# Cosformer attention and a token-channel mixer on one core: first fills in quarters, w_ch1 in rows, the start of w_ch2 in halves

## The chip, the cores and the metric

One core of a Trainium2 chip. The metric is the device time of one execution in microseconds (us); lower is better. The engines are named as in the profile: PE (TensorE, products) with PEld (its weight loads), DVE (VectorE), ACT (ScalarE), POOL (GpSimd), and the queues of SP (SyncE) and POOL that issue DMAs. Inputs and output are float32 in the chip's main memory (HBM); the products run in bfloat16.

## The reference

```python
# q, k, v: (8, 8, 576, 64)
theta = pi / 2 * arange(S) / S
phi(x) = concat([relu(x) * cos(theta), relu(x) * sin(theta)], -1)
kv = einsum('bhsf,bhsd->bhfd', phi(k), v)
z = sum(phi(k), axis=2)
num = einsum('bhsf,bhfd->bhsd', phi(q), kv)
den = einsum('bhsf,bhf->bhs', phi(q), z)[..., None] + 1e-6
x = (num / den), heads side by side        # (8, 576, 512)

h = relu(x.T @ w_tok1) @ w_tok2            # 576 -> 256 -> 576, over tokens
u = x + h.T
out = u + relu(u @ w_ch1) @ w_ch2          # 512 -> 1536 -> 512, over channels
```

## The kernel before

**Tiling.** A sequence of 576 rows is four chunks of 128 rows (row 4p + r of a head lies in partition p, chunk r) and a tail of 64; the tails of two batches share one tile. A batch has a front (features of k and q, the values with a column of ones, key-value products, numerators, the token mixer) and a channel part (`Channel`: `c_main` multiplies by w_ch1 into `c_ps`, ACT applies ReLU into `h1T`, `o_step` multiplies by w_ch2 into `o_ps`, DVE adds u, SP stores). The channel part of batch b runs through a list of steps, and `pieces` gives the pieces of the front of the next batch, each with the step behind which it is put. Nothing is reordered afterwards: each engine executes its instructions in the order in which the program writes them, and waits by semaphores.

**The first front.** Batch 0 has no channel part to lie beside, so `first_front` is written out by hand. It opens with `busy(idle_ps, 12)`: twelve products of the identity with zeros, 512 columns each, whose result nobody reads. Then, for heads 0 to 3 and again for heads 4 to 7, four chunks of q become features and are transposed on PE (`q_trans`, L343), with one such filling product behind each group of four transposes. More of them follow beside the k sums (`ksum`, L287). Then come key-value products (L323), denominators (`dens`, L303), numerators (`num_half`, L371), first token products (`tok1`, L394), transposes of x (`turned_x`, L437) and the second token products (`turned_b`, L444). It ends with the first three blocks of w_ch1's product for batch 0 (`c_block`, L572), with the four blocks of the 512 contraction rows in the outer loop. Every product on PE is two instructions, a weight load and the product.

**The first loads.** SP and ACT load q, k and v of batch 0, and SP the two token weights (as `u_sb` in the profile, since they are staged in buffers of that name). GpSimd loads the weights that are cast on the way to bfloat16: the tail rows of w_tok1 (L185), w_ch1 in four pieces (L190; two halves of its columns, each in two pieces of 256 rows), of which the first waits for k of batch 0, and w_ch2 in three thirds (L198). In the profile both channel weights are called `w_ch`. The loads of batch 1 (k, v, q, each with its tail) are issued by SP, and the first of them waits for w_ch1's second piece. k and q of batch 2 wait for w_ch2's second third.

**Batch 1's front beside batch 0's channel part.** The plan of `pieces` for the first case names, behind step 8, value casts on ACT and GpSimd (`values`, L276 and L278) and the loads of w_ch2:

```python
(8, V, 2, pool), (8, load_w_ch2, 0), (8, V, 3, pool),
(8, load_w_ch2, 1), (8, load_w_ch2, 2), (9, V, 1, act), (9, QS, 0)]
```

V is a value cast, QS the features of a chunk of q. Behind step 11 come the key-value products of batch 1 and the transposes of the first q chunks (QT). The output products of batch 0 follow: chunks 0 and 1 take turns over w_ch2's thirds, two contraction blocks in a step.

Of the kernel before, what the change touches and what calls it, by code (L numbers as in the profile page):

```python
# [16 lines left out]
def kernel(  # L17
# [15 lines left out]
    nc = tc.nc  # L33
# [5 lines left out]
    Dm2, D_ch = moe_w_ch1.shape  # L39
# [143 lines left out]
        nc.gpsimd.memset(t[half(1)], 0.0)  # L183
    for g in range(2):
        nc.gpsimd.dma_start(out=w_tail1[half(g), :], in_=moe_w_tok1[SM:S, :])  # L185
    C2 = D_ch // 2
    w_ch1_done = []
    for c2 in range(2):
        for ki in range(0, NCC, 2):
            w_ch1_done.append(nc.gpsimd.dma_start(  # L190
                out=w_ch1[:, ki:ki + 2, c2 * C2:(c2 + 1) * C2],
                in_=moe_w_ch1[ki * P:(ki + 2) * P, c2 * C2:(c2 + 1) * C2]
                .rearrange("(n c) d -> c n d", c=P)))
    after(w_ch1_done[0], k_done)
    w_ch2_done = []
    def load_w_ch2(third):
        ki = third * NCH // 3
        w_ch2_done.append(nc.gpsimd.dma_start(  # L198
            out=w_ch2[:, ki:ki + 4, :].rearrange("t (a n) d -> t a n d", n=2),
            in_=moe_w_ch2[ki * P:(ki + 4) * P, :].rearrange("(a t n) d -> t a n d", t=P, n=2)))  # L200

    def busy(dst, times):
        for _i in range(times):
            nc.tensor.matmul(dst, ident, zeros[:, 0:dst.shape[-1]], start=True, stop=True)

    def cast_tok1(mi):
        nc.scalar.copy(w_tok1[:, :, mi * P:(mi + 1) * P], w_tok1n[:, :, mi * P:(mi + 1) * P])
# [8 lines left out]
    class Front:  # L218
# [253 lines left out]
        def pieces(self, b, before):  # L472

            first, odd, late = b == 1, b % 2 == 1, b == 2
            V, KV, N = self.values, self.kv, self.num
            KS, QS, QT, T = self.k_side, self.q_side, self.q_trans, self.tok2
            C, O = 0, NCH
            if first:  # L480

                u, act, pool = before.tok2, nc.scalar, nc.gpsimd
                plan = [(2, u, 0, ps_at, False), (2, u, 1, ps_at, False), (3, u, 2, ps_at, False),
                        (4, KS, 0), (4, u, 3, ps_at, False), (5, KS, 1),
                        (5, u, R, ps_at, False), (5, KS, 2, True), (6, KS, 3, True), (7, KS, R),
                        (7, V, R, nc.vector), (8, V, 0, act),
                        (8, V, 2, pool), (8, load_w_ch2, 0), (8, V, 3, pool),
                        (8, load_w_ch2, 1), (8, load_w_ch2, 2), (9, V, 1, act), (9, QS, 0)]
                plan += [(11, KV, ci) for ci in range(NSC)]
                plan += [(11, QS, 1), (11, QS, 2, True), (11, self.kv_out),  # L490
                         (11, QT, 0, (0, H), act, ps_at), (11, QT, 1), (11, QS, R),
                         (O, QT, 2), (O, N, 0), (O, QS, 3), (O + 1, QT, R),
                         (O + 1, N, 1), (O + 3, N, 2), (O + 3, QT, 3),
                         (O + 5, N, R), (O + 7, N, 3), (O + 8, before.tail_cast)]
            else:
                if late:
                    plan = [(C + 5, V, 1, nc.vector), (C + 5, V, 3, nc.vector),
                            (C + 6, V, 0, nc.scalar), (C + 6, V, 2, nc.scalar),
                            (C + 7, V, R, nc.scalar)]
                else:  # L500
                    plan = [(C + at, V, ci, nc.scalar)
                            for ci, at in enumerate((-1, -1, 0, 1, 2))]

                if odd:
                    sides = ((-4, KS, 0), (-3, QS, 0), (0, KS, 1), (0, KS, 2), (1, QS, 1),
                             (1, KS, 3), (1, QS, 2), (2, QS, 3))
                elif late:
                    sides = ((-4, KS, 0), (-3, KS, 1), (0, KS, 2), (1, KS, 3), (1, QS, 0),
                             (2, QS, 1), (3, QS, 2), (4, QS, 3), (5, KS, R), (9, QS, R))
                else:  # L510
                    sides = ((-4, KS, 0), (-3, KS, 1), (0, KS, 2), (1, KS, 3), (1, QS, 0),
                             (2, KS, R), (2, QS, 1), (3, QS, 2), (4, QS, R), (5, QS, 3))
                for at, side, ci in sides:
                    plan.append((C + at, side, ci))
                    if side == QS:
                        plan.append((C + at, self.q_trans_dma, ci))

                plan += [(C + at, KV, ci) for ci, at in
                         enumerate((7, 7, 8, 8, 8) if late else
                                   (2, 3, 4, 5, 6) if odd else (2, 3, 4, 6, 7))]  # L520
                plan.append((C + (8 if late else 6 if odd else 7), self.kv_out))
            if first:
                at, mix, t = (), O + 7, O + 11
            elif odd:
                at, mix, t = (C + 8, C + 9, C + 10, C + 11, O + 2), O + 3, O + 7
            elif late:
                at, mix, t = (C + 10, C + 11, O + 1, O + 2, O + 4), O + 5, O + 9
            else:
                at, mix, t = (C + 9, C + 10, C + 11, O + 1, O + 3), O + 4, O + 8
            plan += [(i, N, ci) for i, ci in zip(at, ORDER)]  # L530
            plan += [(mix, self.mix_head, 0), (mix + 1, self.mix_head, 1),
                     (mix + 2, self.mix_tail)]

            plan += [(t + at, T, ci) for ci, at in enumerate((0, 1, 2, 3, 3) if not first else
                                                             (0, 0, 1, 2, 2))]
            plan += [(t + 3 - first, self.u_trans_dma, 3, R)]
            plan.append((t + 2 - first, self.u_trans_dma, 0, 3))
            if odd:
                plan.append((t + 3 - first, self.tail_trans_dma))
            slots = {}  # L540
            for slot, what, *args in sorted(plan, key=lambda p: p[0]):
                slots.setdefault(slot, []).append((what, args))
            return slots
# [109 lines left out]
    def first_front(f):  # L653
# [1 line left out]

        idle_ps = ps_at.tile([P, 2, 512], F32, name="idle_ps", tag="at")[:, 0, :]
        lo_heads, hi_heads = (0, HH), (HH, H)
        busy(idle_ps, 12)

        for j in range(2):  # L660
            f.feature("q", 3, j, lo_heads, on_act=True)
        for heads in (lo_heads, hi_heads):
            for ci in range(R):
                if (heads, ci) != (lo_heads, 3):
                    f.feature("q", ci, 0, heads)
                    f.feature("q", ci, 1, heads)
                f.q_trans(ci, heads)
                busy(idle_ps, 1)
        f.q_side(R)
        f.q_trans(R, pool=ps_at)  # L670
        busy(idle_ps, 2)
# [98 lines left out]


    results = [dict() for _ in range(B)]
    load_batch(1, "kvq", behind=w_ch1_done[1])
    tails = {0: tail0}
    fronts = {0: Front(0, results[0], tail0)}

# [8 lines left out]
    for b in range(B):  # L785
# [4 lines left out]
        for i, step in enumerate(steps):  # L790
# [3 lines left out]


            if b == 0 and i == NCH:
                load_batch(2, "kq", behind=w_ch2_done[1], tails=False)
            if b == 0 and i == NCH + 13:
                load_batch(2, "v")
                load_batch(2, "k", main=False)  # L800
# [46 lines left out]
```

## Time and profile before

| | |
|---|---|
| median of 3 runs | 268.46 us (267.81 to 268.73) |
| profiled execution | 268.86 us, of which the span from first to last instruction is 267.1 us |
| PE busy | 260.8 us of the span, 2,063 products |
| DVE, ACT, POOL busy | 165.7, 128.0, 12.6 us |
| granted PE clock | full in all 40 slices |
| DMA | 53.68 MB, mean 201 GB/s |
| last output product ends | 263.9 us; the rest is the last addition and store |

The profile is one execution. A group's line gives its start, its length, the engine, the line of the program, the operation, the buffers and how many instructions; in brackets stands the idle time ahead of it and what ended it. "Issue" means that the engine waited for nothing that the profile shows. PE's products are pipelined: one of 512 columns lasts 0.38 us in the list, but the next begins 0.216 us after it. In the DMA view q1 is the queue that SP's loads and stores use, q0 the one of GpSimd's, and q8 carries instructions; each line has packets, megabytes and the share of the 16 DMA engines. A DMA's time is from its issue to its landing, when its semaphore tells of it.

### The profile page before, as it was taken

To read this page: it belongs to the slowest core of one execution; us is meant where nothing else is said; L and a number is where in the kernel's file an instruction comes from. 1 tells how busy PE (TensorE), PEld (TensorE's weight loads), DVE (VectorE), ACT (ScalarE), POOL (GpSimd) and SP (SyncE) were. 2 spreads that over 40 slices of the span, in tenths; PEclk is the share of its full clock that TensorE was granted. 3 is DMA by queue.
4 is the path that set the end of the run, shared out by engine and by line. 5 is a ranking of instruction groups with operands and counts; after the bars stand their busy time and mean duration, and the time that the engine had idled before them with its cause. 6 is when DMAs were issued, how large, how long until landed. Compare 5 with 4: busy or idle time off the path is not lost.

```text
span 267.1 us, 5160 instructions
## 1 busy us (share of the span) xinstructions
PE 260.8 (98%) x2063; PEld 139.6 (52%) x2063; DVE 165.7 (62%) x381; ACT 128.0 (48%) x227; POOL 12.6 (5%) x26
## 2 busy tenths in 40 slices
PE   7989999999999999999999999999999999999995
PEld 2665466465644455446644455446644455445544
DVE  6974888785565846876565846776565846720022
ACT  4963795428506362546516362546606372526500
POOL 6420140000000000000000000000000000000000
PEclk9999999999999999999999999999999999999999
DMA  6999998869998999469994989279964560180023
GB/s 218 338 280 284 330 163 193 306 157 321 177 356 272 290 192 324 120 157 280 149 325 118 290 199 351 80 178 248 247 246 118 157 120 0 47 197 16 2 89 108
DMA packets 91191, 53.68 MB, mean 201 GB/s; under 512 B 59424, under 2 KB 85536, under 8 KB 91168
## 3 DMA queue, kind: packets, MB, share of 16 engines
q1 hardware_dynamic: 88576, 49.62, 69.5%
q0 software_dynamic: 2064, 3.21, 6.8%
q10 hardware_dynamic: 528, 0.52, 0.6%
q8 instruction: 16, 0.26, 0.4%
q14 instruction: 7, 0.06, 0.1%
HBM read 35.85 MB, written 9.44 MB: 170 GB/s over the span
## 4 chain that ended last, share of the span: by engine, by line
PE 84%; DMA 12%; SPq 1%; POOL 1%; issue 0%; DVE 0%
PE o_ps L595 35%; PE c_ps L562 27%; DMA w_ch<-in_moe_w_ch_dram 6%; PE u_ps L418 6%; PE b_ps L394 6%; PE ct_ps L582 4%; DMA vt<-in_v_dram 4%; PE num_ps L371 3%; DMA kt<-in_k_dram 3%; PE kv_ps L323 3%; SPq L86 1%; SPq L92 1%; PE qT_ps L343 1%; POOL v_aug L278 0%; POOL w_ch L190 0%
## 5 line engine op out<-in xcount | busy, mean ns | idle before, releaser
L595 PE MATMUL o_ps<-w_ch,h1T 128*128 128x512 bf16 (+2 forms) x408 | 94.2, 366 | 0.3 <-DMA w_ch<-in_moe_w_ch_dram 0.3
L562 PE MATMUL c_ps<-uT,w_ch 128*128 128x512 bf16 (+2 forms) x384 | 91.6, 372 | 0.0
L566 ACT ACTIVATE h1T<-c_ps 128x512 bf16<-128x512 f32 x93 | 55.3, 598 | 60.0 <-PE c_ps L562 59.8
L595 PEld LDWEIGHTS <-h1T 128*128 128x128 bf16 x408 | 37.6, 97 | 39.9 <-issue 0.6
L562 PEld LDWEIGHTS <-w_ch 128*128 128x128 bf16 x384 | 33.5, 98 | 29.8
L600 DVE TENSOR_TENSOR o_sb<-o_ps,u_sb 128x512 f32<-128x512 f32 (+2 forms) x34 | 22.4, 659 | 29.3 <-PE o_ps L595 29.2
L421 DVE TENSOR_TENSOR u_sb<-u_ps,x_sb 128x512 f32<-128x512 f32 x32 | 21.8, 689 | 8.6 <-PE u_ps L418 8.6
L425 ACT CAST u_bf<-u_sb 128x512 bf16<-128x512 f32 x28 | 17.3, 618 | 16.5 <-DVE u_sb L421 16.4
L418 PE MATMUL u_ps<-B,w_tok 128*128 128x512 bf16 x80 | 22.4, 379 | 0.0
L399 ACT ACTIVATE B<-b_ps 128x512 bf16<-128x512 f32 (+1 forms) x9 | 4.8, 549 | 35.1 <-PE b_ps L394 35.1
L380 DVE TENSOR_TENSOR x_sb<-num_ps,den 128x512 bf16<-128x512 f32 x28 | 19.4, 691 | 1.0
L582 PEld LDWEIGHTS <-w_ch 128*128 128x128 bf16 x192 | 13.9, 98 | 8.7
L394 PE MATMUL b_ps<-x_sb,w_tok 128*128 128x512 bf16 x64 | 17.9, 379 | 0.0
L582 PE MATMUL ct_ps<-uT_tail,w_ch 128*128 128x128 bf16 x192 | 16.9, 219 | 0.0
L265 DVE TENSOR_SCALAR qp<-qt,cos_t 128x512 bf16<-128x512 f32 (+1 forms) x35 | 16.1, 460 | 1.0 <-DMA qt<-in_q_dram 1.0
L265 DVE TENSOR_SCALAR kp<-kt,cos_t 128x512 bf16<-128x512 f32 x32 | 15.5, 489 | 0.4 <-DMA kt<-in_k_dram 0.4
L276 ACT CAST v_aug<-vt 128x512 bf16<-128x512 f32 (+1 forms) x28 | 15.6, 584 | 0.1
L265 DVE TENSOR_SCALAR qp<-qt,sin_t 128x512 bf16<-128x512 f32 (+1 forms) x34 | 15.4, 453 | 0.0
L600 DVE TENSOR_TENSOR o_sb<-o_ps,u_tail 128x512 f32<-128x512 f32 x4 | 2.8, 692 | 19.0 <-PE o_ps L595 19.0
L371 PEld LDWEIGHTS <-qpT 128*128 128x128 bf16 x256 | 11.6, 98 | 4.7 <-issue 0.5
L265 DVE TENSOR_SCALAR kp<-kt,sin_t 128x512 bf16<-128x512 f32 x28 | 13.4, 480 | 0.0
L334 DVE CAST kv_sb<-kv_ps 128x260 bf16<-128x260 f32 x7 | 3.0, 433 | 16.3 <-ACT kv_sb L334 16.3
(95 smaller groups left out, 231.7 us busy)
## 6 DMA issues: line engine op xcount, KB each, us to landing
out_dram<-o_sb SPq DMA_DIRECT2D x31, 256.0 KB, 3.1
kt<-in_k_dram SPq DMA_DIRECT2D x7, 1024.0 KB, 6.6
vt<-in_v_dram SPq DMA_DIRECT2D x7, 1024.0 KB, 6.8
qt<-in_q_dram SPq DMA_DIRECT2D x7, 1024.0 KB, 8.8
w_ch<-in_moe_w_ch_dram POOLq DMA_DIRECT2D x4, 384.0 KB, 10.1
w_ch<-in_moe_w_ch_dram POOLq DMA_DIRECT2D x3, 512.0 KB, 8.2
out_dram<-o_sb SPq DMA_DIRECT2D x9, 128.0 KB, 2.3
qtt<-in_q_dram SPq DMA_DIRECT2D x8, 128.0 KB, 5.5
```

The costliest lines, as they stand in the source:

```text
L265: nc.vector.tensor_scalar(o_ap, i_ap, scalar1=w, scalar2=0.0, op0=ALU.mult, op1=ALU.max)
L371: nc.tensor.matmul(num_ps[:, g, j * DP:j * DP + D1], self.qT_of(ci, g * HH + j), self.kv_sb[g][:, j, 0:D1], start=True, stop=True)
L380: nc.vector.tensor_mul(self.x_of(ci)[rows].rearrange("p (g j d) -> p g j d", g=2, j=HH)[:, lo:hi], nv[:, :, :, 0:D], den[:, lo:hi].to_broa ...
L394: nc.tensor.matmul(self.b1_ps[mi], w, self.x_of(ci), start=(ci == ORDER[0]), stop=(ci == ORDER[-1]))
L418: nc.tensor.matmul(u_ps, w_tok2[:, ki, ci * P:(ci + 1) * P], self.B1[:, ki, :], start=(ki == 0), stop=(ki == NT - 1))
L421: nc.vector.tensor_add(u, u_ps[rows], self.x_of(ci)[rows])
L425: nc.scalar.copy(self.ub[:, ci, :], u)
L562: nc.tensor.matmul(c_ps[:, lo:hi], w_ch1_of[:, ki, mi // 2, mi % 2, :], uT[:, lo // P:hi // P, ki, :], start=(ki == 0), stop=(ki == NCC - 1))
L566: nc.scalar.activation(self.h1T[:, mi, :], c_ps, AF.Relu)
L582: nc.tensor.matmul(self.ct_ps[:, mi % R, :], w_ch1_of[:, ki, mi // 2, mi % 2, :], self.tail.uT[:, ki, :], start=(mi % R == 0 and ki == 0), ...
L595: nc.tensor.matmul(o_ps, h, w_ch2[:, ki, cols], start=ki == 0, stop=ki == NCH - 1)
L600: nc.vector.tensor_add(o_sb, o_ps, u)
```

## The change

`busy` can make a filling product as several of fewer columns. The twelve at the start and the four behind the transposes of heads 0 to 3 are made as four of 128 columns each. w_ch1 is loaded in four pieces of 128 whole rows, one for each block of the contraction. w_ch2's first third is loaded as two halves of two contraction blocks each. The first half stands ahead of GpSimd's cast of value chunk 2, and waits for v of batch 1; the second stands between the casts of chunks 2 and 3. k and q of batch 2 wait for the same middle third as before, which is now the third load of w_ch2.

```diff
--- before.py
+++ after.py
@@ -183,27 +183,26 @@
         nc.gpsimd.memset(t[half(1)], 0.0)
     for g in range(2):
         nc.gpsimd.dma_start(out=w_tail1[half(g), :], in_=moe_w_tok1[SM:S, :])
-    C2 = D_ch // 2
     w_ch1_done = []
-    for c2 in range(2):
-        for ki in range(0, NCC, 2):
-            w_ch1_done.append(nc.gpsimd.dma_start(
-                out=w_ch1[:, ki:ki + 2, c2 * C2:(c2 + 1) * C2],
-                in_=moe_w_ch1[ki * P:(ki + 2) * P, c2 * C2:(c2 + 1) * C2]
-                .rearrange("(n c) d -> c n d", c=P)))
+    for ki in range(NCC):
+        w_ch1_done.append(nc.gpsimd.dma_start(out=w_ch1[:, ki, :],
+                                              in_=moe_w_ch1[ki * P:(ki + 1) * P, :]))
     after(w_ch1_done[0], k_done)
     w_ch2_done = []
-    def load_w_ch2(third):
-        ki = third * NCH // 3
+    def load_w_ch2(lo, hi, behind=None):
         w_ch2_done.append(nc.gpsimd.dma_start(
-            out=w_ch2[:, ki:ki + 4, :].rearrange("t (a n) d -> t a n d", n=2),
-            in_=moe_w_ch2[ki * P:(ki + 4) * P, :].rearrange("(a t n) d -> t a n d", t=P, n=2)))
-
-
-
-    def busy(dst, times):
-        for _i in range(times):
-            nc.tensor.matmul(dst, ident, zeros[:, 0:dst.shape[-1]], start=True, stop=True)
+            out=w_ch2[:, lo:hi, :].rearrange("t (a n) d -> t a n d", n=2),
+            in_=moe_w_ch2[lo * P:hi * P, :].rearrange("(a t n) d -> t a n d", t=P, n=2)))
+        if behind is not None:
+            after(w_ch2_done[-1], behind)
+
+
+
+    def busy(dst, times, parts=1):
+        n = dst.shape[-1] // parts
+        for i in range(times * parts):
+            lo = i % parts * n
+            nc.tensor.matmul(dst[:, lo:lo + n], ident, zeros[:, 0:n], start=True, stop=True)
 
     def cast_tok1(mi):
         nc.scalar.copy(w_tok1[:, :, mi * P:(mi + 1) * P], w_tok1n[:, :, mi * P:(mi + 1) * P])
@@ -484,8 +483,9 @@
                         (4, KS, 0), (4, u, 3, ps_at, False), (5, KS, 1),
                         (5, u, R, ps_at, False), (5, KS, 2, True), (6, KS, 3, True), (7, KS, R),
                         (7, V, R, nc.vector), (8, V, 0, act),
-                        (8, V, 2, pool), (8, load_w_ch2, 0), (8, V, 3, pool),
-                        (8, load_w_ch2, 1), (8, load_w_ch2, 2), (9, V, 1, act), (9, QS, 0)]
+                        (8, load_w_ch2, 0, 2, v_landed), (8, V, 2, pool), (8, load_w_ch2, 2, 4),
+                        (8, V, 3, pool), (8, load_w_ch2, 4, 8), (8, load_w_ch2, 8, NCH),
+                        (9, V, 1, act), (9, QS, 0)]
                 plan += [(11, KV, ci) for ci in range(NSC)]
                 plan += [(11, QS, 1), (11, QS, 2, True), (11, self.kv_out),
                          (11, QT, 0, (0, H), act, ps_at), (11, QT, 1), (11, QS, R),
@@ -655,7 +655,7 @@
 
         idle_ps = ps_at.tile([P, 2, 512], F32, name="idle_ps", tag="at")[:, 0, :]
         lo_heads, hi_heads = (0, HH), (HH, H)
-        busy(idle_ps, 12)
+        busy(idle_ps, 12, parts=4)
 
         for j in range(2):
             f.feature("q", 3, j, lo_heads, on_act=True)
@@ -665,7 +665,7 @@
                     f.feature("q", ci, 0, heads)
                     f.feature("q", ci, 1, heads)
                 f.q_trans(ci, heads)
-                busy(idle_ps, 1)
+                busy(idle_ps, 1, parts=4 if heads == lo_heads else 1)
         f.q_side(R)
         f.q_trans(R, pool=ps_at)
         busy(idle_ps, 2)
@@ -770,7 +770,7 @@
 
 
     results = [dict() for _ in range(B)]
-    load_batch(1, "kvq", behind=w_ch1_done[1])
+    v_landed = load_batch(1, "kvq", behind=w_ch1_done[1])[1]
     tails = {0: tail0}
     fronts = {0: Front(0, results[0], tail0)}
 
@@ -794,7 +794,7 @@
 
 
             if b == 0 and i == NCH:
-                load_batch(2, "kq", behind=w_ch2_done[1], tails=False)
+                load_batch(2, "kq", behind=w_ch2_done[2], tails=False)
             if b == 0 and i == NCH + 13:
                 load_batch(2, "v")
                 load_batch(2, "k", main=False)
```

## The prediction

> **What bounds the kernel now.** I read the page's busy table, then the list of what PE waited for, the windows, the chain of waits and the timelines of the first 47 us.
>
> ```profile
> span 267.1 us, 5160 instructions
> ...
> PE 260.8 (98%) x2063; PEld 139.6 (52%) x2063; DVE 165.7 (62%) x381; ACT 128.0 (48%) x227; POOL 12.6 (5%) x26
> ```
>
> PE is idle for 6.3 us. By the windows it is busy for 216.48 of the 216.50 us between 46.5 and 263.0, so nothing can be won there, and what is won before 46.5 lasts to the end. PE's own waits:
>
> ```profile
> PE num_ps L371 <- issue: 0.9, 1, 0.9
> PE o_ps L595 <- DMA w_ch<-in_moe_w_ch_dram: 0.3, 1, 0.3
> ```
>
> The first is this hole in PE's timeline, in the middle of eight products on one buffer, where the instruction that is late waits for no semaphore:
>
> ```profile
> 18.26 0.19 PE L371 MATMUL num_ps<-kv_sb,qpT_tail 128*128 128x65 bf16 x1
> 19.36 0.39 PE L371 MATMUL num_ps<-kv_sb,qpT_tail 128*128 128x65 bf16 x7 [0.91 <-issue]
> ```
>
> The DMA view of 16.5 to 18 us has the first packet of a queue that carries instructions:
>
> ```profile
> q8 instruction: 1, 0.02, 3.9%
> ```
>
> It ran from 16.91 to 17.84 with 16,384 bytes. The page counts 4,126 PE instructions (products and loads) and that queue has 16 packets in all: some 258 each, a block of about 256. I read the hole as PE out of instructions until that block was usable. In PE's order, 445 instructions stand before the hole.
>
> The second wait is the end of this chain:
>
> ```profile
> 22.04 10.38 DMA vt<-in_v_dram
> 32.42 0.05 issue
> 32.48 0.92 POOL v_aug L278
> 33.40 5.86 DMA w_ch<-in_moe_w_ch_dram
> 39.26 0.04 issue
> 39.30 0.59 PE o_ps L595 x2
> ```
>
> GpSimd casts a value chunk as soon as v of batch 1 has landed, only then issues w_ch2's first third, and the first output product waits for it. By start times the wait is 0.50 us (last transpose 38.74, its pitch 0.055, next start 39.30).
>
> **Part 1: fills as four.** 12 + 4 fills of 512 columns become 64 of 128: 48 more products and 48 more loads, 96 instructions, all ahead of the hole. The columns are the same. Transposes of 128 columns with a load each run at a pitch of 0.055 us, four in 0.22, against 0.216 for one 512-column product: nothing.
>
> ```profile
> 1.37 4.49 PE L206 MATMUL idle_ps<-zeros,ident 128*128 128x512 bf16 x12 [1.37 <-POOL ident masks.py:199]
> 6.07 0.40 PE L343 MATMUL qT_ps<-ident,qp 128*128 128x128 bf16 x4 [0.21 <-DVE qp L265]
> ```
>
> Until 4.8 us fills start every 0.427 us, and loads take 0.15. If a load were not hidden behind 128 columns there (0.107), 23 of 48 would be done when the rate doubles and the rest end 0.6 us later; PE's waits for qp until 7.5 us and 0.32 us before the tail's transposes (10.09) take that up. So 0 at both ends.
>
> What it moves is the block's edge: the 445th instruction is now what was the 349th, in the denominators at 16.01 us. The request moves too. Room for the block comes when PE enters the one before it, 256 instructions earlier, or some 51 ahead of that (the packet at 232.84 began 51 instructions before its edge). Before: 13.4 us, or 11.5 with the lead; usable 19.36, so 6.0 to 7.8 us later. After: the same instruction count is reached at 9.1, or 7.4 with the lead, giving 15.1 to 15.2: 0.8 us ahead of need. The hole goes; its price lies between 0 and 0.91, and I take 0.91, since the slowest of the other packets, 0.8 us slower than this one, would still cost only 0.1. Later edges are 250 instructions of some 0.1 us from their request and show no hole now.
>
> What is late next? Buffers and DVE: the last x chunk comes at 20.22 + 0.06 for a product due at 20.23. That leaves 0.86 us.
>
> **Part 2: w_ch1 in whole rows.** Four issues of about 0.8 us on GpSimd, as before; 512 packets of 3,072 bytes for 1,024 of 1,536. By the packet rows (1,536 in 134 ns, 2,048 in 173) a 3,072 one takes some 251 ns against 268: 6% of 7.75 us, 0.45 us. If a row were split into packets as now, 0. PE's instructions already wait for all four pieces by the fourth contraction block (26.11; the last lands at 25.4), so the new layout needs nothing sooner; 0.86 earlier makes that 25.25, and it costs 0.15 if the pieces are no faster, 0 otherwise. The second piece, which releases batch 1's loads, is half of w_ch1 as before (20.97), so k, v and q come 0 to 0.4 us sooner.
>
> **Part 3: w_ch2.** The first half waits on v, as the cast behind it did, and is issued at 32.1 to 32.5 instead of 33.40. Queued behind it on GpSimd are both value casts, pushed by about 0.65 us (the 32 KB tail issues took 0.60, the 512 KB ones 0.72): they end by 35.6, and the key-value products on these chunks, due at 37.18, now 36.3, do not wait. The second half is issued near 33.4 to 34.4, the other thirds at 35.1 to 36.5; packets run at full rate some 2 us after an issue ends (34.12, full at 36), so the queue does not run dry. All of w_ch2 shifts by 0.7 to 1.2 us. First half: 1.4 us of packets, landed at 37.4 to 38.1. Batch 2's k and q, behind the same middle third, shift alike.
>
> The fixed part of a DMA speaks against halves. The Trainium skill ("DMA: Bandwidth & Descriptors", Anatomy of one DMA) gives about 2.0 us fixed per DMA; paid again by the second half, the estimate would be no gain. Here w_ch1's four pieces, issued 0.8 us apart, land at 19.1, 20.97, 22.85 and 25.4, which is their packets' time: in a row the fixed part is paid once.
>
> **The sum.** The first output product is due at 38.80 - 0.86 = 37.94. Batch 1's q lands at 35.9 and its second chunk's features end at 37.85; with the transposes that allows 38.36, or 38.0 if q comes 0.4 sooner. So it starts at 38.0 to 38.4 for 39.30: 0.9 to 1.3. The next bound is the middle third: landed at 43.09, its product started at 43.16; it now lands 0.7 to 1.2 sooner. The least of these is 0.8 to 1.1; I take 0.95. On the profiled execution (span 267.1, time 268.86) that is a span of 266.15; on the median of the three runs, 268.46, it is 267.5. Half of the forecast's own cases lie in 267.3 to 267.7, nearly all in 267.1 to 267.8.
>
> **Rivals.**
> - The hole is not fetch, or moves without closing (0.12). Then only the 0.50 us goes: 267.95. For it: the block had landed at 17.84, 1.5 us before PE went on. Against: no semaphore, the packet's time, the count. The Trainium skill ("Runtime: NRT & Kernel Launch", Instruction fetch mechanics) has blocks of 256 instructions and says that crossing one is "mostly hidden", with room for 2,048 instructions on PE; the count of 256 agrees, but a packet came when PE had done some 410, and 0.91 us was not hidden.
> - The middle third comes no sooner, because the second half pays its own way from issue to first packet (some 2 us) and the queue runs dry meanwhile (0.08). PE then waits at 43.1 as it does now, and only 0.1 is left: 268.4.
> - Slower: the first half overtakes the end of q (0.10). Its packets take 173 ns and q's 18 to 46, and each engine has eight of them: 1.4 us in front of q's last packets. q then lands at 37.3, its second features end 1.95 later, and the first output product starts at 39.7 for 39.30: 268.9; behind both halves 270.3. It decides if q lands after 36.9. Against: at 33 us q1's packets are mostly small tails, so q is nearly through.
> - The clock rises a step later because short fills count for less (0.03): some 1 us slower, 269.5. For it nothing in the profile; the granted clock of every slice is full.
>
> The forecast keeps 0.67. A measurement of this kernel tells about 0.3% (0.8 us, below 267.65) from no change. Of the 0.67 some 0.58 is below that; with scatter of the runs and the first rival's low side, 0.60 faster. Slower by over 0.8 us are the bad half of the third rival, the fourth, and a block that comes still later: 0.11. The rest, 0.29, is no change. The range takes in the first two rivals and gains up to 1.5: 266.9 to 268.6.
>
> **What would show it.** Right: no hole by issue between 14 and 24 us; the first instruction packet at 12 to 14 us; GpSimd's first w_ch2 issue ahead of its casts; the first o_ps product at 38.0 to 38.4 and the middle third landed by 42.4; PE full afterwards. Wrong: a hole of over 0.3 us in the denominators; q landing after 36.9; PE waiting for w_ch2 more than 0.3 us; a wait of the fourth contraction block on w_ch1; a first transpose later than 6.3.

## The result, and the profile after

The changed kernel takes 270.98 us (median of 16 runs, 269.40 to 273.51) beside 268.45 us for the kernel before (16 runs, 267.81 to 269.58). The ratio is 1.0074, with an interval of 1.0054 to 1.0094. On a second chip it was 270.44 beside 268.70, 1.0056 [1.0037, 1.0076]. The forecast was 267.5 us, in 266.9 to 268.6: the sign was wrong. (Where executions are counted one by one below, the few whose granted clock was 0.994 or less are left out.)

The profiled execution took 271.16 us. Its page, to be set beside the first fence of the prediction:

```profile
span 269.4 us, 5236 instructions
...
PE 259.8 (96%) x2090; PEld 143.1 (53%) x2111; DVE 166.2 (62%) x381; ACT 127.9 (47%) x227; POOL 11.7 (4%) x27
```

PE does the same work within 1 us and is idle for 9.6 us, 3.3 more. The list of what PE waited for (in total, times, longest) says where:

```profile
PE t_ps L443 <- ACT B L398: 1.8, 1, 1.8
PE num_ps L370 <- DMA qpT_tail<-qp_tail: 1.5, 1, 1.5
```

The hole by issue and the wait for w_ch2 have left the list, as forecast, and two waits that the kernel before did not have have entered it.

**What came as forecast.** The DMA view of 12 to 14.2 us has the first instruction packet (12.64 to 13.69; 16.91 to 17.84 before):

```profile
q8 instruction: 1, 0.02, 3.0%
```

In PE's timeline the numerators that held the hole run through:

```profile
18.54 0.40 PE L370 MATMUL num_ps<-kv_sb,qpT_tail 128*128 128x65 bf16 x8
...
23.61 1.25 PE L443 MATMUL t_ps<-w_tok,B 128*128 128x512 bf16 x5 [1.80 <-ACT B L398]
```

At the end of that first line (18.94 us; 19.75 before) PE is 0.8 us ahead of the kernel before; at the second line (22.44 before) it is 1.17 behind. GpSimd's first issue for w_ch2 stands ahead of its cast (33.49 in place of 33.40, since v itself now lands at 33.20 in place of 32.42), its first half lands at 38.80, the middle third at 42.54 in place of 43.12, and no output product waits.

**The first loss.** The chain of waits from 9 to 26 us leads from PE's wait back to one DMA:

```profile
9.94 12.03 DMA u_sb<-in_moe_w_tok_dram
21.96 0.02 issue
21.99 1.09 ACT w_tok L211
23.08 0.20 ACT w_tok L213
23.28 0.29 ACT B L398
23.57 0.05 issue
23.61 1.90 PE t_ps L443 x8
```

This is the load of w_tok2 (issued at L119), which landed at 18.83 before and at 21.96 now. ACT casts it, and the ReLU that makes B is queued behind the two casts; PE's `turned_b` needs B. In ACT's timeline of the kernel before the same cast stands here:

```profile
18.85 1.12 ACT L212 CAST w_tok<-u_sb 128x512 bf16<-128x512 f32 x1 [1.45 <-DMA u_sb<-in_moe_w_tok_dram]
```

From the landing to PE's product the chain above takes 1.65 us. As far as w_tok2 goes, PE could by the same steps have gone on at 20.48 in the kernel before, and it did at 22.44: w_tok2 had 1.96 us to spare. In the changed kernel PE was ready 0.63 us sooner (21.81), and w_tok2 came 3.13 us later. That makes the 1.80 us.

**The second loss.** The chain from 68 to 77 us:

```profile
71.12 4.36 DMA qpT_tail<-qp_tail
75.48 0.05 issue
75.53 0.42 PE num_ps L370 x8
```

Batch 2's transposes of the tails of q (a DMA) took 4.36 us. In the kernel before they took 2.80 (70.26 to 73.06), and PE used them at 73.22. In the DMA view of 70 to 74.5 us there is now an instruction packet, which ran from 73.29 to 74.29; in the kernel before the nearest ones were at 66.50 and 79.09. The view's line for the transposes (from issue to landing) before, and its two lines now:

```profile
qpT_tail<-qp_tail SPq DMA_TRANSPOSE x1, 2.8
```

```profile
q8 instruction: 1, 0.02, 1.4%
...
qpT_tail<-qp_tail SPq DMA_TRANSPOSE x1, 4.4
```

Of the last 32 small writes of 4 bytes on SP's queue ahead of the landing, thirty start by 73.46 and two at 74.28 and 74.29, as the packet ends. The landing is reported at 75.48; what the last 1.2 us went into these rows do not show.

The windows put both losses in their places (stretch, its length, PE busy and instructions, clock, DMA share, GB/s), first before:

```profile
17.00:25.00 8.00, 7.01 (x71) 1.00 1.14 239
...
72.00:77.00 5.00, 5.00 (x46) 1.00 0.87 267
```

and after:

```profile
17.00:25.00 8.00, 6.06 (x72) 1.00 1.04 231
...
72.00:77.00 5.00, 3.42 (x46) 1.00 0.88 237
```

Between and behind these two stretches PE's start times run parallel in the two kernels. The changed one is 1.18 us late from 24 us on, 0.68 from the first output product on (there the kernel before waits for w_ch2), 0.62 from 44 to 72, and 2.31 from there to the end.

### The profile page after: what moved, and what is told of

Read it like the earlier page. It is cut to its first block, busy times and chain, and to the rows that moved or that the text cites. A ratio compares the mean times of both kernels' runs of the same rounds, so it can differ in the third digit from the quotient of the medians.

```text
span 269.4 us, 5236 instructions
## 1 busy us (share of the span) xinstructions
PE 259.8 (96%) x2090; PEld 143.1 (53%) x2111; DVE 166.2 (62%) x381; ACT 127.9 (47%) x227; POOL 11.7 (4%) x27
## 4 chain that ended last, share of the span: by engine, by line
PE 84%; DMA 6%; DVE 4%; SPq 3%; issue 1%; ACT 1%
PE o_ps L595 33%; PE c_ps L562 27%; PE u_ps L417 7%; PE b_ps L393 6%; DMA u_sb<-in_moe_w_tok_dram 4%; PE ct_ps L582 4%; PE kv_ps L322 3%; DVE x_sb L379 2%; PE num_ps L370 2%; SPq L86 2%; DMA qpT_tail<-qp_tail 2%; PE c_ps L572 1%; SPq L92 1%; PE qT_ps L342 1%; DVE den L364 1%; DVE den L365 1%
## 5 line engine op out<-in xcount | busy, mean ns | idle before, releaser
L595 PE MATMUL o_ps<-w_ch,h1T 128*128 128x512 bf16 (+2 forms) x392 | 92.7, 366 | 0.6
L424 ACT CAST u_bf<-u_sb 128x512 bf16<-128x512 f32 x28 | 17.3, 618 | 16.5 <-DVE u_sb L420 14.8
L264 DVE TENSOR_SCALAR kp<-kt,cos_t 128x512 bf16<-128x512 f32 x32 | 16.4, 517 | 0.0
L370 PE MATMUL num_ps<-kv_sb,qpT 128*128 128x65 bf16 x256 | 13.0, 193 | 0.1
```

Of the source, the lines that this page charges most:

```text
L264: nc.vector.tensor_scalar(o_ap, i_ap, scalar1=w, scalar2=0.0, op0=ALU.mult, op1=ALU.max)
L370: nc.tensor.matmul(num_ps[:, g, j * DP:j * DP + D1], self.qT_of(ci, g * HH + j), self.kv_sb[g][:, j, 0:D1], start=True, stop=True)
L424: nc.scalar.copy(self.ub[:, ci, :], u)
L595: nc.tensor.matmul(o_ps, h, w_ch2[:, ki, cols], start=ki == 0, stop=ki == NCH - 1)
```

## The experiments

Part 1 is the fills, part 2 w_ch1 in whole rows, part 3 w_ch2's halves. Theories at the start: C, that whole rows of w_ch1 crowd out w_tok2; F, that the 96 more PE instructions put an instruction packet beside the transposes. In the expectations C is called P at first; the rival of P is R, and that of F is V. A ratio is to the kernel before on the same chip, with its 95% interval.

### Parts one by one

**e1_fills_halves**, the changed kernel with w_ch1 as before:

```diff
-    for ki in range(NCC):
-        w_ch1_done.append(... out=w_ch1[:, ki, :], ...)
+    for c2 in range(2):
+        for ki in range(0, NCC, 2):
+            w_ch1_done.append(... out=w_ch1[:, ki:ki + 2, c2 * C2:(c2 + 1) * C2], ...)
```

> The change without its second part: fills in quarters and w_ch2 in halves, w_ch1 in two column halves as before. Theory P (w_ch1's packets of 3,072 bytes take turns with those of the token weights and push w_tok2's landing from 18.8 to 22.0 us; ACT's cast of w_tok2 then holds up its ReLU of B, and PE waits 1.8 us): w_tok2 lands at 18.5 to 19.5, no wait ahead of the second token products, the hole by issue stays closed, about 267.5 us, or 268.0 if q of batch 1 still lands after 37. Rival R (w_tok2's landing scatters by itself, or is late because the instruction block or the fills moved): w_tok2 lands after 21 here too and PE waits over 1 us, about 270.

Measured: 1.0028 [1.0006, 1.0050], 269.32 us. Its profile is its slowest execution, 271.09: w_tok2 landed at 18.77 and PE did not wait at t_ps, but for 1.2 us at num_ps, with an instruction packet at 73.33 beside the transposes, and 1.0 at o_ps. The median is neither theory C's (267.5 to 268.0) nor its rival's (270).

**e2_fills**, part 1 alone:

```diff
-        busy(idle_ps, 12)
+        busy(idle_ps, 12, parts=4)
...
-                busy(idle_ps, 1)
+                busy(idle_ps, 1, parts=4 if heads == lo_heads else 1)
```

> Fills in quarters alone. Theory P: the hole of 0.9 us by issue is gone, the first instruction packet comes at 12 to 14 us, w_tok2 lands at 18.5 to 19.5; PE then waits 1.2 to 1.4 us for w_ch2's first third instead of 0.5, so 268.2 to 268.6, no change. Rival R: w_tok2 after 21, a wait of over 1 us ahead of the second token products, 269.5 or more. Were the hole not instruction fetch, it would stand behind the 541st instruction and the time would be 268.4 too, but with the hole in the profile.

Measured: 0.9994 [0.9971, 1.0017], 268.25 us. The profile (267.88) has no hole, w_tok2 at 19.38, and the instruction packet at 76.32, behind the transposes. PE waited 0.3 us for w_ch2, not the 1.2 to 1.4 that were expected.

**e3_rows**, part 2 alone:

```diff
-            w_ch1_done.append(... out=w_ch1[:, ki:ki + 2, c2 * C2:(c2 + 1) * C2], ...)
+        w_ch1_done.append(... out=w_ch1[:, ki, :], ...)
```

> w_ch1 in whole rows alone. Theory P: the hole stays at 18.4 to 19.4 us, w_tok2 lands at 21.5 to 22.5, PE waits about 1.0 us more ahead of the second token products (due at 22.44), batch 1's v lands 0.8 later and with it w_ch2: 269.3, or up to 271 if the transposes of batch 2's q tail, which had 0.2 us to spare, are late too. Rival R: w_tok2 at 18.5 to 19.5 and about 268.3, since rows alone neither move the instruction block nor PE.

Measured: 1.0010 [0.9994, 1.0027], 268.72 us. The profile (267.42) has no wait at t_ps, and no hole either, although the fills are as before: its first packet runs at 15.57. What is unlike the two kernels of the question is GpSimd's first issue for w_ch1, here and in the kernel before:

```profile
10.05 5.31 POOL L188 DMA_DIRECT2D w_ch<-in_moe_w_ch_dram  x4 [5.13 <-DMA kt<-in_k_dram]
```

```profile
10.58 3.21 POOL L190 DMA_DIRECT2D w_ch<-in_moe_w_ch_dram  x4 [5.66 <-DMA kt<-in_k_dram]
```

Both wait for the keys. In e3 the first of the four issues alone lasts from 10.05 to 13.70, until 0.46 us after DVE is through with its features of k (9.99 to 13.24); in the kernel before it lasts 0.84, beside the same DVE work. I call the first *held*. DVE's first k feature began 0.06 us ahead of the issue in e3; in the kernel before, 0.19. With w_ch1 behind the keys it began 0.01 to 0.11 us ahead in the four profiles that are held, and 0.12 to 0.19 in the nine that are not. The Trainium skill ("DMA: Bandwidth & Descriptors", SWDGE vs HWDGE vs iDMA) says that GpSimd writes the descriptors of its DMAs into memory from which DVE locks it out in some of its modes. The held issues agree with that; the issues of 0.55 to 0.84 us beside the same operations show that it isn't so in every execution. Since this profile is held, e3 does not decide between C and its rival.

**e4_halves**, part 3 alone:

```diff
-                        (8, V, 2, pool), (8, load_w_ch2, 0), (8, V, 3, pool),
-                        (8, load_w_ch2, 1), (8, load_w_ch2, 2), (9, V, 1, act), (9, QS, 0)]
+                        (8, load_w_ch2, 0, 2, v_landed), (8, V, 2, pool), (8, load_w_ch2, 2, 4),
+                        (8, V, 3, pool), (8, load_w_ch2, 4, 8), (8, load_w_ch2, 8, NCH),
+                        (9, V, 1, act), (9, QS, 0)]
...
```

> w_ch2's first third in halves alone. Theory P: hole as before, w_tok2 at 18.5 to 19.5; the first half is issued at 32.4 and lands by 38.5, the wait of 0.5 us for it goes: 267.95. If its packets push q of batch 1 from 35.97 to beyond 36.9, the first output product waits for q's transposes instead: 268.3 to 268.9. Rival R says nothing else here: 267.95.

Measured: 0.9985 [0.9968, 1.0001], 268.51 us; the profile is held too (w_tok2 at 16.89, no hole). Alone no part costs or gains anything that is clear of the scatter. The pairs:

**e5_rows_halves** and **e6_fills_rows**, the changed kernel without part 1 and without part 3:

```diff
 e5
-        busy(idle_ps, 12, parts=4)
+        busy(idle_ps, 12)
...
 e6
-                        (8, load_w_ch2, 0, 2, v_landed), (8, V, 2, pool), (8, load_w_ch2, 2, 4),
+                        (8, V, 2, pool), (8, load_w_ch2, 0), (8, V, 3, pool),
...
```

> Rows and halves, fills as before (no extra PE instructions). Theory F (the 96 extra instructions move an instruction-block fetch of PE from 79 to 73 us, beside the transposes of batch 2's q tail; its 1 us packet holds up the last of them, and PE waits 1.2 to 1.5 us): the fetch stays at 77 to 79 us, the tail's transposes land 2.6 to 3.0 us after issue, no wait there, 268.3 to 269.5 by whether w_ch1 gets ahead of the token weights. Rival V (the tail's transposes are late because batch 2's loads and w_ch1's rows move): PE waits over 1 us for the tail's transposes here too, about 270.5.

> Fills and rows, w_ch2 as before. Theory F: the fetch comes near 73 us whenever PE is about as late as in the changed kernel; then PE waits 1.2 to 1.5 us for the tail's transposes and the time is 270 to 271, otherwise 268 to 269: a wide spread, median 269 to 270.5. Rival V (w_ch2's halves are needed for the loss): narrow, 268 to 269, no such wait.

Measured: e5 1.0001 [0.9977, 1.0025]; e6 1.0050 [1.0019, 1.0080]. e5's profile (270.08) is not held and has the first loss (w_tok2 at 22.12, 1.0 us at t_ps) and the hole (0.7 us). e6's (269.00, the fastest of its 12) is held, has w_tok2 at 17.30, and the second loss:

```profile
PE num_ps L369 <- DMA qpT_tail<-qp_tail: 1.4, 1, 1.4
```

with a packet at 71.09 beside transposes that ran from 68.90 to 73.33. So the two losses come apart: each profile may have one, both or none. Both medians lie where F expects them, and F's rival V, by which e6 would lie at 268 to 269, falls.

### Each loss attacked

**e7_phase**, the changed kernel with 260 more PE instructions than before in place of 96, so that each block of 256 ends about where it did:

```diff
-        busy(idle_ps, 12, parts=4)
+        busy(idle_ps, 12, parts=8)
...
-                busy(idle_ps, 1, parts=4 if heads == lo_heads else 1)
+                busy(idle_ps, 1, parts=8 if heads == lo_heads else 2)
...
```

> The changed kernel with its fills cut finer still (eighths, and some later fills in halves and quarters), so that 260 instead of 96 PE instructions are added: block edges fall 4 instructions from where they fell before the change. Theory F: the packet beside batch 2's tail transposes is gone (77 to 80 us), PE does not wait there, the median falls by 1.0 to 1.7 to 269.3 to 270. Rival V: the wait of 1.2 to 1.5 us stays, 270.5 to 271.5.

Measured: 1.0040 [1.0013, 1.0067], 270.05 us. The profile has the transposes at 2.80 us and no wait for them, but w_tok2 at 22.53 and 1.8 us at t_ps. That is just above what F expects (269.3 to 270), and F alone fails: more than half of the loss is still there with the blocks moved.

**e8_after_late**, the changed kernel with w_ch1 behind the last v of batch 0:

```diff
-    load_main(vt0, v, 0, HH, H)
+    v0_done = load_main(vt0, v, 0, HH, H)
...
-    after(w_ch1_done[0], k_done)
+    after(w_ch1_done[0], v0_done)
```

> The changed kernel with one wait changed: the first w_ch1 piece waits for batch 0's last v load (some 14 us) instead of k. Theory C (w_ch1's 3,072-byte packets take turns with the token weights when GpSimd issues them at 10.2 us, and not when its issue is held up behind DVE until 13.7 to 14.2, as in three of the single-part runs): w_tok2 lands at 16 to 18, PE does not wait ahead of the second token products, 1.0 to 1.5 us faster than the changed kernel: 267.3 where the tail's transposes are in time, 269 where not. Without C: w_tok2 still after 20 and about 271, or w_ch1's last piece so late (over 26) that PE waits for it.

Measured: 1.0070 [1.0042, 1.0097], 270.77 us. The wait at t_ps has gone (w_tok2 at 17.81), and this has come in its place:

```profile
PE c_ps L572 <- DMA w_ch<-in_moe_w_ch_dram: 1.1, 1, 1.1
PE o_ps L595 <- DMA w_ch<-in_moe_w_ch_dram: 0.6, 1, 0.6
```

The first issue went at 15.49 in place of 10.23, the last piece of w_ch1 landed at 26.91 in place of 25.07, and everything behind it is late too. I had moved w_ch1 too far; the run speaks neither for C nor against it. The next four issue it at 12.31 to 13.99, for e9 2.1 us later in place of 5.3.

**e9_after_v1**, **e10_phase_v1**, **e11_before_v1**, **e12_rows_halves_v1**: the changed kernel, e7, the kernel before and e5, each with w_ch1 behind the first half of batch 0's v:

```diff
-    load_main(vt0, v, 0, 0, HH)
+    v0_done = load_main(vt0, v, 0, 0, HH)
...
-    after(w_ch1_done[0], k_done)
+    after(w_ch1_done[0], v0_done)
```

> The changed kernel, with w_ch1's first load held until the first half of batch 0's values has landed (12.1 us) in place of the keys (10.0). Theory of the two coincidences (whole rows that start early crowd out the token weights, worth 1.0 to 1.8 us at t_ps; and an instruction packet beside batch 2's transposes of the tails of q, worth 1.2 to 1.5): the first is taken away and the second stays, so w_tok2 lands before 19.5, PE does not wait at t_ps, and the median is 0.2 to 0.4% above before instead of 0.7. Rival, instruction blocks alone: as the changed kernel, 0.7% above. Rival, the first loads alone: no slower than before, 0.1% faster or more.

> As the run before, and with 260 more PE instructions than the kernel before instead of 96, so that the blocks' edges fall again about where they fell in it. Theory of the two coincidences: both are gone, and the hole by issue too; PE waits at neither t_ps nor num_ps, and the median is 0 to 0.4% under before. Instruction blocks alone: as e7, 0.4% above before. First loads alone: as the run before this, no slower than before. If it stays 0.3% or more above before with neither wait in its profile, a third cost is there that has no name yet.

> The kernel before, with w_ch1's first load held until the first half of batch 0's values has landed. Theory: w_ch1 no longer lies ahead of the instruction packet and of the token weights, so the hole of 0.9 us by issue goes without any of the three parts of the change and w_tok2 lands before 18; w_ch1's last piece lands no later than 25.8, which the products stood without a wait in the runs before. Median 0.2 to 0.4% under before. Rival, the hole does not hang on w_ch1's packets: within 0.1% of before. Rival, w_ch1 becomes late: a wait at c_ps, 0.2% or more above.

> The second and third part of the change without the fills, and w_ch1's first load held in the same way. Theory: whole rows cost time only where they start early, so PE does not wait at t_ps and the time that e5 lost is back: 0.2 to 0.5% under before, 267.5 to 268.2 us. Rival, rows and halves cost in another way: as e5, within 0.1% of before.

Measured: e9 0.9985 [0.9963, 1.0008], e10 0.9991 [0.9974, 1.0008], e11 0.9990 [0.9974, 1.0006], e12 0.9979 [0.9960, 0.9998]. Two lines take the changed kernel from 0.6 to 0.7% slower to level with the kernel before. GpSimd's timeline of e9:

```profile
12.31 3.17 POOL L188 DMA_DIRECT2D w_ch<-in_moe_w_ch_dram  x4 [7.38 <-DMA vt<-in_v_dram]
```

w_tok2 lands at 18.15, w_ch1's last piece at 25.03, no later than in the changed kernel: nothing was gained by the early start. What PE waited for has no t_ps any more:

```profile
PE num_ps L370 <- DMA qpT_tail<-qp_tail: 0.5, 1, 0.5
PE qT_ps L342 <- DVE qp_tail L264: 0.2, 1, 0.2
```

The theory's figure for e9, with the second loss still there 0.2 to 0.4% above, was too high: e9 came out as its rival says, by which the first loads alone do it, and e10, with the blocks moved as well, is no faster. e11 has no hole in its profile though none of the three parts is in it (packet at 16.19), but its median moved by only 0.1%, and its profile waits 0.7 us for other transposes instead. e12 is at the low end of what was expected (0.2 to 0.5% under).

### Packets, fills and repeats

**e13_short_packets**, the changed kernel with the same early start and the same order of pieces, but each row written to two places:

```diff
-    w_ch1 = const.tile([P, NCC, D_ch], BF16, name="w_ch1")
+    w_ch1 = const.tile([P, 2, NCC, D_ch // 2], BF16, name="w_ch1")
...
-        w_ch1_done.append(nc.gpsimd.dma_start(out=w_ch1[:, ki, :],
-                                              in_=moe_w_ch1[ki * P:(ki + 1) * P, :]))
+        w_ch1_done.append(nc.gpsimd.dma_start(out=w_ch1[:, :, ki, :],
+                                              in_=moe_w_ch1[ki * P:(ki + 1) * P, :]
+                                              .rearrange("c (h d) -> c h d", h=2)))
```

> The changed kernel with its four whole-row pieces of w_ch1 in the same order and waiting for the same keys, but with each row written to two places, so that the packets have 1,536 bytes again. Theory that the packets' length crowds out the token weights: w_tok2 lands before 20 even where GpSimd's issue is not held, PE does not wait at t_ps for more than 0.3, and the median is 0 to 0.4% above before. Rival, the early start or the order of the pieces does it whatever the packets: w_tok2 lands at 21.5 or later where the issue is not held, and the median is 0.6 to 0.8% above before as in the changed kernel.

Measured: 1.0016 [0.9990, 1.0043], 268.75 us; the profile (267.67) is not held, w_tok2 lands at 20.01, and PE waits for nothing behind its start. So it came as the theory of the packets' length says; the changed kernel on the same chip was 1.0056 (e15, below). The two queues in the DMA view of 15 to 19 us (packets, MB, share of the 16 engines), in the changed kernel:

```profile
q0 software_dynamic: 209, 0.59, 74.7%
q1 hardware_dynamic: 203, 0.46, 32.6%
```

and in e13:

```profile
q0 software_dynamic: 431, 0.64, 88.0%
q1 hardware_dynamic: 165, 0.35, 25.7%
```

w_ch1 moves at nearly the same rate in both, with twice the packets in e13. In the changed kernel one of its packets (3,072 bytes) takes 247 ns, in e13 (1,536) 135, and one of w_tok2's (2,304) 106 in both. From 17 to 18 us the changed kernel starts 49 packets of w_ch1 and 48 of w_tok2, so they take turns, nearly one for one; of each pair of turns w_tok2 gets 106 of 353 ns, with short packets 106 of 241. By 18 us e13 has 5 packets of w_tok2's size left to start in the next microsecond, the changed kernel 43. The Trainium skill ("DMA: Bandwidth & Descriptors", Queues, rings and completion order) says that a DMA engine goes round its queues packet by packet; these counts agree. One thing e13 does not separate: its four issues take 3.55 us in all and those of the changed kernel 2.35, and w_ch1 starts 0.3 us later (first packet at 14.58 for 14.27).

The landing hangs on the last few packets. In e13 the last eight of w_tok2's 256 start some 0.2 us apart (18.10 to 19.50), in e5 the last seven 0.33 apart (19.59 to 21.57): turns of what looks like one late DMA engine, shared with short packets in e13 and with long ones in e5. What made it late is not shown, but an instruction packet fits. With 96 more instructions the first one runs at 11.9 to 13.1 us, ahead of w_tok2, and the last packet of w_tok2 starts 1.3 to 3.4 us after nine tenths of them have (ten profiles); in e3, e4, e11, e12 and e18 it comes at 15.5 to 16.2, when w_tok2 is nearly through, and that is 0.3 to 0.9 us.

**e14_fills_rows_v1**, e6 with w_ch1 behind the first half of v:

```diff
-    after(w_ch1_done[0], k_done)
+    after(w_ch1_done[0], v0_done)
```

> First and second part of the change, with w_ch1's first load held until the first half of batch 0's values has landed. Theory that the loss of e6 (0.5%) came by the first loads: 0 to 0.3% under before. Rival, the fills lose by instruction packets whatever the first loads do: 0.3% or more above before, with a wait of 1.2 us or more at num_ps for the transposes of the tails of q.

Measured: 1.0005 [0.9981, 1.0029], 268.60 us (e6: 1.0050). The profile (267.83) has w_tok2 at 19.77 and no wait. The median lies between the two expectations, nearer to the first.

**e15_after_again** and **e16_after_look**, the changed kernel itself:

```diff
 (no edit)
```

> The changed kernel again. Theory: 0.6 to 0.8% above before; in the profile GpSimd's first w_ch1 load is not held, w_tok2 lands after 21 and PE waits 1 to 2 us at t_ps; with a second wait at num_ps over 1 us the time is near 271, without it near 269.5. If its profile shows w_tok2 before 20 and a time of 270.5 or more, the loss is elsewhere.

> The changed kernel once more, for its profile alone: the same as the run before this, w_tok2 after 21 where the first load of w_ch1 is not held and before 19 where it is, and a time that less the waits of PE in the list is 267 to 268.4, as in the ten profiles of before.

Measured: e15 1.0056 [1.0037, 1.0076], 270.44 us; e16 one execution of 270.00 us. The two profiles are not held, with w_tok2 at 21.32 and 22.42 and 1.1 and 1.6 us at t_ps, and both are without the second loss (packets at 78.4). e15's profile, 268.86, is the fastest of its twelve.

**e17_short_phase** and **e18_rows_halves_v1_again**, e13 with e7's fills, and e12 unchanged:

```diff
 e17
-        busy(idle_ps, 12, parts=4)
+        busy(idle_ps, 12, parts=8)
...
 e18
 (no edit)
```

> e13 (the changed kernel with w_ch1's packets short again) with 260 more PE instructions than the kernel before in place of 96. Theory that the upper group of e13 (5 of 12 executions at 270.06 or more, the others at 268.83 or less) comes of an instruction packet beside batch 2's transposes: the upper group goes, at most 1 of 12 is 1.2 us or more above the middle of the rest, and the median is 267.9 to 268.6. Rival, the upper group has another cause, in the first loads for instance: 3 or more of 12 at 270 or more again.

> e12 again: second and third part of the change, w_ch1's first load held until the first half of batch 0's values has landed. Theory: 0.1 to 0.4% under before as in e12 (0.9979). If it is within 0.05% of before or above it, e12 was a fortunate draw.

Measured: e17 1.0014 [0.9992, 1.0035], 268.97 us, with 2 of 12 executions at 270.4, the others at 269.52 or less: between what theory and rival expected, and inconclusive. Its profile is one of the two (270.38), and its largest loss is not the transposes (2.76 us long) but the old hole, by the second instruction packet at 17.39, which the larger count has moved there:

```profile
19.80 0.39 PE L397 MATMUL b_ps<-x_sb,w_tok 128*128 128x512 bf16 x1 [0.97 <-issue]
```

e18 is 0.9991 [0.9975, 1.0007], 268.27 us. With e12 (0.9979) that is the best version found, but the gain of 0.1 to 0.2% is under what a measurement of this kernel can tell.

### All profiles together

| profiles | w_tok2 lands | PE waits at t_ps |
|---|---|---|
| whole rows, behind the keys, not held (after, e5, e7, e15, e16) | 21.32 to 22.53 | 1.0 to 1.8 us, all five |
| short packets, behind the keys, not held (before, e2, e13, e17) | 18.83 to 20.01 | none |
| behind the keys, held (e1, e3, e4, e6) | 16.07 to 18.77 | none |
| behind v (e8 to e12, e14, e18) | 16.48 to 19.77 | none |

In all twenty profiles the time less PE's listed waits (without the one for `ident` at the start) is 266.9 to 268.4 us, while the times run from 267.42 to 271.16. So the waits in PE's list make up most of the difference.

That an instruction packet makes the transposes of the tails of q late can be read from all profiles, which have three such DMAs each. Of these 60, 45 took 2.76 to 3.19 us and 15 took 3.68 to 4.53. The 15 are just those at which an instruction packet started between 0.3 us ahead of the issue and 2.3 us behind it. At most of them PE had time to spare; in the profiles of the changed kernel, e1 and e6 it had not.

For the second loss I count executions more than 1.2 us above the median of the kernel before, among the versions whose profile is without the first loss: 1 of 60 with the fills as before (e3, e4, e11, e12, e18), 11 of 56 with 96 more instructions (e1, e2, e9, e13, e14), 2 of 23 with 260 more (e10, e17). Of the kernel before it is 3 of 157. In the changed kernel itself five of e15's executions lie at 269.68 to 270.05 us and five at 270.84 to 271.08, so there the second loss may be more frequent; no profile shows one of these five.

## Why the prediction was wrong

- **Part 2 is the step that failed.** It took 0 to 0.45 us as a gain and asked one question of w_ch1: who needs it sooner. It did not ask what else is on the DMA engines while w_ch1 loads. The answer lay in the profile of before: w_tok2 landed at 18.83 in the middle of w_ch1's packets, with 1.96 us to spare, and part 1 was to take 0.86 of that away. The term is a loss of 1.0 to 1.8 us at t_ps, in all five profiles with whole rows that start early. Two runs each take away one condition: a later start (e9, 0.9985) and shorter packets (e13, 1.0016); the held issue of e3 and e6 shows the same, by chance and in one execution each. The prediction priced a packet's bytes and duration rightly (251 ns forecast, 247 measured) and drew the wrong thing from it: w_ch1's packets took some 8% less time in all, but 83% more per turn. Two smaller things were wrong as well: the issues took 0.54 to 0.74 us, not 0.8, and batch 1's loads went 0.84 us later, not 0 to 0.4 sooner.
- **In the median the loss needs the fills too.** Rows without the fills are 1.0010 (e3) and 1.0001 (e5), rows with them 1.0040 to 1.0074 (e6, e7 and the changed kernel), fills without rows 0.9994 and 1.0028 (e2, e1). The prediction added its parts up as if each stood alone. Two reasons fit: without the fills PE comes later to t_ps, by the hole where there is one, and the early instruction packet of the fills can make one DMA engine late ahead of w_tok2. No run separates them.
- **No rival held it.** The rival on the slower side looked at the end of q under w_ch2's first half and set a mark, q landing after 36.9. q did land at 37.46 in the changed kernel, but it had been issued late: batch 1's first load went at 21.82 in place of 20.98, behind w_ch1's second piece. In e9, with the same halves, q lands at 35.39. The mark was passed for another reason, and the mechanism is not borne out.
- **Part 1 was right for the profiled execution, and too large for the median.** The hole has gone in every profile with 96 more instructions, and PE was 0.8 us ahead behind it (forecast 0.86). That the hole is PE's instructions coming late fits all profiles: the three that have one (before, e5, e17) have an instruction packet that starts between 16.91 and 17.39, and no other profile has one there. But e3, e4, e11, e12 and e18 have no hole either, without the fills. Their first packet ran at 15.53 to 16.19; it was at 16.91 and 17.33 in before and e5, which have it. The term of 0.86 us was the price of one execution, not of the median: e2, whose profile is without the hole, is 0.9994 of before.
- **"Later edges show no hole now" missed the other half of part 1.** The later edges still do not stop PE for instructions. But an instruction packet, about 1.0 us long, makes transposes beside it land 0.5 to 1.8 us later, and at 73 us those of the tails of q had 0.16 us to spare. In three profiles (the changed kernel, e1, e6) this cost 1.2 to 1.5 us. That it comes in about a fifth of the executions with 96 more instructions is what the count suggests; no run took that packet away by itself, so its share of the median is open.
- **Part 3 held as worked out,** with everything 0.8 us later because v was: first issue ahead of the casts, no wait at the first output product, the middle third 0.6 us sooner. Alone it is 0.9985 [0.9968, 1.0001], which is not clear of 1.
- **"What is won before 46.5 lasts to the end" holds in some executions only.** Without the first loss the forecast of the front comes true: e9's first output product starts at 38.17 (forecast 38.0 to 38.4) and its middle third lands at 42.20 (by 42.4). e13 is 1.20 us ahead of the kernel before at 44 and 1.18 at the end. But e9 is 0.91 ahead at 43.2 and 0.25 from 73 on: it arrives earlier at the transposes and waits for them there. PE's full windows hid how little was to spare.
- **The forecast gain is in the median of no version:** the lowest ratios (e12, e4, e9) are 0.15 to 0.21% under the kernel before, where 0.35% was forecast.

## What to carry to other kernels

Before you change the size or the start of a transfer's packets, list everything that lands while it runs, with the time each has to spare: queues that take turns share by packet, so longer packets slow the other queue even when the total gets shorter. A wait of under 1 us that one profile shows, in a kernel whose runs scatter by as much, is a price for that execution, so look at a second profile before you put it into a sum. A weight that is needed late is best started as late as it can be, behind the loads that are needed first: here 2.1 us later cost nothing (e9) and 5.3 us later cost as much as it saved (e8).

## What was not expected of the hardware

- GpSimd's first issue for w_ch1 took 0.55 to 0.84 us in nine of the thirteen profiles in which it waits for the keys, and 3.6 to 3.7 us in four. The long ones ended 0.46 to 0.48 us after DVE's last feature of k. With them w_tok2 landed at 16.07 to 18.77 and PE did not wait for it.
- One instruction packet of 16,384 bytes takes 0.9 to 1.8 us, mostly about 1.0. A DMA transpose with such a packet beside it landed after 3.7 to 4.5 us in place of 2.8 to 3.2, in 15 cases of 15.
- 96 more instructions on PE moved the instruction packets: the first from 15.5 to 17.3 us (seven profiles with the fills as before) to 11.9 to 13.1 (ten profiles), the sixth from 77.5 to 80.8 us to 71.1 to 78.4. In the changed kernel itself the sixth came at 73.29 once and at 78.4 twice.
